# One expert's four result blocks share the tile that held its transposed rows, in place of two rotating buffers

## The chip, the cores and the metric

The kernel runs on one core of a Trainium2 chip. The metric is the time of one execution in microseconds (us), the median of repeated runs. A core has a matrix engine (PE, with its weight loads shown apart as PEld), a vector engine (DVE), an activation engine (ACT), GpSimd (POOL) and a queue engine (SP). Each runs its own list of instructions in order, and an instruction that must wait holds up all that stand behind it on its engine. DMA transfers are issued by SP and POOL and land later.

## The reference

Three stages follow one another: chunked attention, a mixture of experts that sends each of 4608 rows to one of eight experts, and a feed-forward stage with a rational activation.

```python
attn = softmax(scale * q_c @ k_c.T)            # chunks of 64
x    = (attn @ v_c) as rows                     # (4608, 512)
e    = argmax(x @ w_gate, axis=1)
for e in range(8):
    h = maximum(x[mask_e] @ w1[e], 0.0)         # 512 -> 1024
    out[mask_e] = gate_w * (h @ w2[e])          # 1024 -> 512
h = out @ w_in                                   # 512 -> 2048
g = (a0 + a1 h + a2 h^2 + a3 h^3) / (1 + |b0||h| + |b1| h^2 + 1e-6)
y = g @ w_out
```

## The kernel before

Rows are handled in tiles of 128. Each expert e takes the first 512 of its rows, in four tiles j = 0 to 3; what an expert has beyond 512 is worked through by `Extra` objects of 128 rows, one of them woven into each expert (`ex`, called `late` once the next expert has begun). Every matrix product is made of three passes over a value split into a high and a low part (`mm3`), so a group of four 128-deep steps is 12 matmuls.

The rows of an expert are gathered by POOL (`g`), transposed on PE, and written by ACT (high part) and DVE (low part) into `xT`, a tile of 16 KB per partition (`prep_x`, called as `p(j)`). There are two places for it, the pools `xt_p[0]` and `xt_p[1]`, and expert e uses `xt_p[e % 2]`; so `xT` of expert e+1, written in the middle of expert e, takes the place that expert e-1 used. `first(c)` makes 128 of the 1024 hidden values for all 512 rows, `relu(c)` moves them out on ACT and DVE as `hT`, and `second(c)` adds their part to four accumulators in PSUM, `yp[0..3]`. `xT` is read for the last time in `first(7)`.

`out(j)` copies `yp[j]` out of PSUM, on DVE for j = 0 and 2 and on ACT for j = 1 and 3, and POOL then scatters the 128 rows to `ys` in DRAM by an indirect DMA. The copy goes to a buffer of the pool `o_p`, which has two buffers that are used in turn; the results of the `Extra` objects (`yos`) and a small work tile for their indices (`extra_idx`) take theirs from the same two. `out(0)` and `out(1)` stand at the end of expert e, `out(2)` behind `first(0)` and `out(3)` behind `first(1)` of expert e+1. The last expert calls all four at its end, and the third and fourth then take buffers of `xg_p`, a pool of three that the gathered rows and the hidden values of the `Extra` (`hrs`) share:

```python
    for j in range(4):
        cur.second(6, (j,))
        cur.second(7, (j,))
        weight(V)
        cur.out(j, j > 1)
```

The order of the instructions on PE, DVE and ACT in this part is that of the program text (a manual schedule). POOL and SP are ordered by the framework's planner, which also puts in the waits. `weight()` splits a block of weights that SP has loaded into its parts (ACT, then DVE); `convert(1)` does half of a conversion of the last stage's weights on DVE. After the experts, `load_rows(0)` reads the first 512 rows of `ys` back into `xt_p[1]`, and the feed-forward stage begins.

Of the kernel before, what the change touches and what calls it, by code (L numbers as in the profile page):

```python
# [9 lines left out]
F32 = mybir.dt.float32  # L10
# [32 lines left out]
def kernel(  # L43
# [31 lines left out]
    xt_p = [ctx.enter_context(tc.tile_pool(name="xt_a", bufs=1))]  # L75
# [155 lines left out]
    def weight(eng=None):  # L231
        raw, tag, ws, c, nm, deint = raws.pop(0)
        ws[c] = split_w(raw, tag, nm, deint,
                        eng or alternate(c if type(c) is int else c[1]))
        ahead()
# [9 lines left out]
    def scatter(idx, o, alone=False):  # L245
        d = nc.gpsimd.indirect_dma_start(
            out=ys, out_offset=bass.IndirectOffsetOnAxis(ap=idx, axis=0), in_=o, in_offset=None)
        if not alone:
            tc.declare_no_dep(d.ins, group="ys", reason="each place has a row of its own")
            tc.add_to_no_dep_group("ys", d.ins)  # L250
# [14 lines left out]
    def new_x(e):  # L265
        return xt_p[e % 2].tile([128, 2, 4, 512], F32R, tag="xt", name=f"xT{e}")
# [34 lines left out]
    def new_out(nm, spare):  # L301
        if spare:
            return xg_p.tile([128, 512], F32, tag="xg", name=nm)
        return o_p.tile([128, 512], F32, tag="o", name=nm)
# [4 lines left out]
    class Extra:  # L309


        def __init__(self, idx, weights, nm, xt=None):
            self.idx, self.nm, self.xt = idx, nm, xt
            self.own = xt is None
            self.w1s, self.w2s = weights
            self.hts, self.hrs = [], []
# [40 lines left out]
        def out(self):  # L357
            o = new_out(f"yo{self.nm}", False)
            nc.scalar.activation(o, self.yp, AF.Copy)
            scatter(self.idx[:, 0:1], o, self.nm == "d")  # L360

    class Expert:


        def __init__(self, e, xt, weights, n):
            self.e, self.xt, self.n = e, xt, n
            self.w1s, self.w2s = weights
            self.yp, self.hts, self.hps = None, {}, {}

        def first(self, c):  # L370
            w = 128 * self.n
# [21 lines left out]
                mm3(self.yp[j], lambda x: ht[:, x, 128 * j:128 * j + 128],  # L393
                    lambda y: w[:, y, i0:i0 + 512], c == 0, c == 7)

        def out(self, j, spare=False):
            o = new_out(f"yo{self.e}_{j}", spare)
            if j % 2:
                nc.scalar.activation(o, self.yp[j], AF.Copy)
            else:  # L400
                V.tensor_copy(o, self.yp[j])
            scatter(sidx[:, self.e, j:j + 1], o)
# [83 lines left out]
    with man:  # L486
# [303 lines left out]
        cur = None  # L790
# [24 lines left out]
        for i in range(NTILE + 1):  # L815
# [64 lines left out]
            if i == X0:  # L880
                cur = Expert(0, new_x(0), (weights0[0:4], weights0[4:8]), EARLY // 128)
# [208 lines left out]
        xt = new_x(1)  # L1090
# [25 lines left out]
        old, cur = cur, Expert(1, xt, (w1s[1], w2s[1]), 4)  # L1116
# [38 lines left out]
        for e in range(1, NE):  # L1155
            nxt = e + 1 < NE
            if e > 1:
                old, cur = cur, Expert(e, xt, (w1s[e], w2s[e]), 4)
# [32 lines left out]
            if nxt:  # L1191
                xt = new_x(e + 1)
# [64 lines left out]
        for j in range(4):  # L1257
            cur.second(6, (j,))
            cur.second(7, (j,))
            weight(V)  # L1260
            cur.out(j, j > 1)


        rows0 = list(load_rows(0))
# [95 lines left out]
```

## Time and profile before

| | |
|---|---|
| median of 3 runs | 1517.3 us (1515.2 to 1517.8) |
| the profiled execution, its own time | 1519.63 us |
| its span, from the first to the last instruction | 1517.2 us |
| mean granted PE clock over the span | 0.989 |
| PE busy | 1463.4 us (96%) |
| DVE busy | 1270.8 us (84%) |
| ACT busy | 926.3 us (61%) |
| POOL busy | 447.9 us (30%) |

The profiled execution took 2.43 us more than its span, and 2.3 us more than the median. Attention fills the first 200 us, the experts the time to about 690 us, the feed-forward stage the rest. Busy shares are averages over these stages; PE's share counts matmuls from start to modelled end, which overlap.

### The profile page before, as it was taken

To read this page: it belongs to the slowest core of one execution; us is meant where nothing else is said; L and a number is where in the kernel's file an instruction comes from. 1 tells how busy PE (TensorE), PEld (TensorE's weight loads), DVE (VectorE), ACT (ScalarE), POOL (GpSimd) and SP (SyncE) were. 2 spreads that over 40 slices of the span, in tenths; PEclk is the share of its full clock that TensorE was granted. 3 is DMA by queue.
4 is the path that set the end of the run, shared out by engine and by line. 5 is a ranking of instruction groups with operands and counts; after the bars stand their busy time and mean duration, and the time that the engine had idled before them with its cause. 6 is when DMAs were issued, how large, how long until landed. Compare 5 with 4: busy or idle time off the path is not lost. (4 is left out here: it accounts for less than half of the span.)

```text
span 1517.2 us, 22399 instructions
## 1 busy us (share of the span) xinstructions
PE 1463.4 (96%) x7812; PEld 1198.8 (79%) x7812; DVE 1270.8 (84%) x2271; ACT 926.3 (61%) x1480; POOL 447.9 (30%) x415
## 2 busy tenths in 40 slices
PE   7999899999999999997899999999999999999998
PEld 5787788877778777876678888888888888888886
DVE  4888776988989889975989888888888888888886
ACT  5888544543444434544667667676776766667675
POOL 5565532121121211112642323222222222222232
PEclk9999999999999999999999999999999999999999
DMA  8999636776767878762301000010100001000000
GB/s 215 250 261 282 175 113 211 249 248 232 256 221 240 252 224 263 226 210 80 97 17 54 1 29 21 0 53 4 42 14 29 29 1 49 8 35 1 28 1 28
DMA packets 122897, 180.07 MB, mean 119 GB/s; under 512 B 51872, under 2 KB 78496, under 8 KB 122784
## 3 DMA queue, kind: packets, MB, share of 16 engines
q1 hardware_dynamic: 112352, 148.20, 32.6%
q0 software_dynamic: 10432, 30.44, 5.6%
q8 instruction: 62, 1.02, 0.3%
q14 instruction: 51, 0.42, 0.1%
HBM read 140.68 MB, written 37.91 MB: 118 GB/s over the span
## 5 line engine op out<-in xcount | busy, mean ns | idle before, releaser
L262 PE MATMUL f<-yT,wf 128*128 128x512 f32 x1728 | 412.8, 390 | 5.7 <-DVE t L449 2.2
L262 PE MATMUL z<-wf,g 128*128 128x512 f32 x1680 | 405.8, 392 | 9.5 <-POOL g L462 4.7
L262 PEld LDWEIGHTS f<-yT,wf 128*128 128x128 f32 x1728 | 323.2, 188 | 74.2 <-DVE t L449 2.7
L262 PEld LDWEIGHTS z<-wf,g 128*128 128x128 f32 x1680 | 314.6, 189 | 77.6 <-POOL g L462 6.4
L462 POOL TENSOR_TENSOR g<-t,g 128x512 fp32r<-128x512 f32 x140 | 209.6, 1498 | 521.3 <-ACT g L461 504.6
L262 PE MATMUL h<-xT,w 128*128 128x512 f32 (+1 forms) x768 | 187.6, 394 | 12.2 <-DVE hT L382 12.2
L262 PE MATMUL y<-w,hT 128*128 128x512 f32 x744 | 183.8, 395 | 0.0
L262 PEld LDWEIGHTS h<-xT,w 128*128 128x128 f32 x768 | 145.7, 193 | 41.9 <-DVE hT L382 14.5
L446 DVE TENSOR_TENSOR t<-t,f 128x512 f32<-128x512 f32 x144 | 98.5, 684 | 90.5 <-ACT u L445 90.0
L448 ACT ACTIVATE u<-t,cq 128x512 f32<-128x512 f32 x144 | 104.6, 726 | 92.0 <-DVE t L447 91.6
L447 DVE SCALAR_TENSOR_TENSOR t<-t,co,u 128x512 f32<-128x512 f32 x144 | 158.9, 1104 | 0.0
L262 PEld LDWEIGHTS y<-w,hT 128*128 128x128 f32 x744 | 136.9, 188 | 27.8 <-issue 0.4
L461 ACT ACTIVATE g<-t 128x512 fp32r<-128x512 f32 x140 | 89.0, 636 | 102.9 <-DVE t L453 102.8
L443 ACT ACTIVATE t<-f,co 128x512 f32<-128x512 f32 x144 | 112.0, 778 | 34.4 <-PE f L262 17.7
L381 ACT ACTIVATE hT<-h 128x512 fp32r<-128x512 f32 (+1 forms) x64 | 37.4, 584 | 148.7 <-PE h L262 106.9
L453 DVE SCALAR_TENSOR_TENSOR t<-t,co 128x512 f32<-128x512 f32 x144 | 125.3, 870 | 2.0
L451 DVE SCALAR_TENSOR_TENSOR t<-t,u 128x512 f32<-128x512 f32 x144 | 102.2, 710 | 15.4 <-ACT u L450 15.4
L452 DVE SCALAR_TENSOR_TENSOR t<-t,u 128x512 f32<-128x512 f32 x144 | 109.1, 758 | 0.5
L445 ACT ACTIVATE u<-f,co 128x512 f32<-128x512 f32 x144 | 98.4, 683 | 14.0 <-DVE t L452 9.8
L449 DVE SCALAR_TENSOR_TENSOR t<-t,co,f 128x512 f32<-128x512 f32 x144 | 106.3, 739 | 0.0
L450 ACT ACTIVATE u<-u 128x512 f32<-128x512 f32 x144 | 90.5, 629 | 2.2
L444 ACT ACTIVATE t<-f 128x512 f32<-128x512 f32 x144 | 85.1, 591 | 0.0
(203 smaller groups left out, 1981.1 us busy)
## 6 DMA issues: line engine op xcount, KB each, us to landing
raw_w<-in_moe_w_dram SPq DMA_DIRECT2D x64, 512.0 KB
raw_s<-in_moe_w_dram SPq DMA_DIRECT2D x64, 512.0 KB
v<-in_v_dram SPq DMA_DIRECT2D x144, 64.0 KB
xs<-x POOLq DMA_DIRECT2D x36, 256.0 KB
out_dram<-o SPq DMA_DIRECT2D x36, 256.0 KB
raw<-in_moe_w_in_dram SPq DMA_DIRECT2D x32, 256.0 KB
raw<-in_moe_w_out_dram SPq DMA_DIRECT2D x32, 256.0 KB
yg<-ys SPq DMA_DIRECT2D x32, 256.0 KB
```

Source lines behind the costliest of these rows:

```text
L262: nc.tensor.matmul(o, lhsT=lhs(x), rhs=rhs(y), start=(first and n == 0), stop=(last and n == 2))
L443: nc.scalar.activation(p, hp, AF.Identity, scale=a3, bias=a2)
L445: nc.scalar.activation(vv, hp, AF.Abs, scale=b0)
L446: V.tensor_tensor(out=p, in0=p, in1=hp, op=ALU.mult)
L447: V.scalar_tensor_tensor(qq, qq, b1, vv, op0=ALU.mult, op1=ALU.add)
L448: nc.scalar.activation(r, qq, AF.Abs_reciprocal_sqrt, bias=cq)
L449: V.scalar_tensor_tensor(p, p, a1, hp, op0=ALU.add, op1=ALU.mult)
L450: last_act = nc.scalar.activation(r, r, AF.Square).ins
L451: V.scalar_tensor_tensor(qq, qq, CQ, r, op0=ALU.add, op1=ALU.mult)
L452: V.scalar_tensor_tensor(qq, qq, -2.0, r, op0=ALU.add, op1=ALU.mult)
L453: V.scalar_tensor_tensor(p, p, a0, qq, op0=ALU.add, op1=ALU.mult)
L462: nc.gpsimd.tensor_tensor(out=gt[:, 1], in0=p, in1=gt[:, 0].bitcast(F32), op=ALU.subtract)
```

## The change

`out(j)` no longer takes a buffer of `o_p` or `xg_p`. The first `out` of an expert asks the pool `xt_p[e % 2]` for a tile of [128, 4, 512] under the same tag as `xT`, that is, for the place of the expert's own `xT`, and each of the four copies writes its quarter of it.

```diff
-            self.yp, self.hts, self.hps = None, {}, {}
+            self.yp, self.ot, self.hts, self.hps = None, None, {}, {}
...
-        def out(self, j, spare=False):
-            o = new_out(f"yo{self.e}_{j}", spare)
+        def out(self, j):
+
+            if self.ot is None:
+                self.ot = xt_p[self.e % 2].tile([128, 4, 512], F32, tag="xt", name=f"yo{self.e}")
+            o = self.ot[:, j]
             if j % 2:
                 nc.scalar.activation(o, self.yp[j], AF.Copy)
...
-            cur.out(j, j > 1)
+            cur.out(j)
```

PE, DVE, ACT and SP keep the order of their instructions; what differs on them is the waits. On DVE, at the end of expert 1 and the start of expert 2, the rows were these (a `waits` note names the semaphores: DMASW are those of POOL's DMAs, DMAHW those of SP's):

```order
L401 COPY yo_0_4453<-y_0_3897 128x512 [waits DMASW4_49,DMASW2_49]
L177 TENSOR_SCALAR cv_4459<-raw_55_4381 128x256 [waits DMAHW6_49,DMAHW5_49]
L178 TENSOR_SCALAR cv_4459<-cv_4459 128x256 [waits DVE_49]
L179 TENSOR_SCALAR cv_4459<-cv_4459 128x256 [waits DVE_49]
L180 SCALAR_TENSOR_TENSOR cv_4459<-raw_55_4381,cv_4459 128x256 [waits DVE_49]
L401 COPY yo_2_4479<-y_2_3899 128x512 [waits DMASW5_49,Activation_49]
L140 TENSOR_TENSOR s_2_0_4482<-raw_s_2_0_4336,s_2_0_4482 128x1024 [waits DMAHW3_49,PE_49,Activation_49]
```

In the change the same place on DVE reads:

```order
L404 COPY yo_4451<-y_0_3895 128x512
L177 TENSOR_SCALAR cv_4456<-raw_55_4379 128x256 [waits DMAHW6_49,DMAHW5_49]
L178 TENSOR_SCALAR cv_4456<-cv_4456 128x256 [waits DVE_49]
L179 TENSOR_SCALAR cv_4456<-cv_4456 128x256 [waits DVE_49]
L180 SCALAR_TENSOR_TENSOR cv_4456<-raw_55_4379,cv_4456 128x256 [waits DVE_49]
L404 COPY yo_4451<-y_2_3897 128x512
L140 TENSOR_TENSOR s_2_0_4478<-raw_s_2_0_4334,s_2_0_4478 128x1024 [waits DMAHW3_49,PE_49,Activation_49]
```

The two copies stand where they stood, without a wait. The waits for scatters are found at a later place instead: where ACT and DVE write the first tile of the `xT` that takes the place next.

POOL is the one engine whose order differs. From the last gather of expert 1's middle (`xgs`) to that of expert 2's, it was:

```order
L240 DMA xgs_4207<-xs,ixs_3985 128x512
L240 DMA xg_0_4689<-xs,gidx 128x512
L240 DMA xg_1_4691<-xs,gidx 128x512
L246 DMA ys<-yo_1_4456,sidx 45568x512
L246 DMA ys<-yo_0_4453,sidx 45568x512
L240 DMA xg_2_4693<-xs,gidx 128x512
L246 DMA ys<-yo_2_4479,sidx 45568x512
L246 DMA ys<-yo_3_4518,sidx 45568x512
L246 DMA ys<-yos_4609,ixs_3985 45568x512
```

and is now:

```order
L240 DMA xgs_4205<-xs,ixs_3983 128x512
L246 DMA ys<-yo_4451,sidx 45568x512
L240 DMA xg_0_4684<-xs,gidx 128x512
L240 DMA xg_1_4686<-xs,gidx 128x512
L246 DMA ys<-yo_4451,sidx 45568x512
L240 DMA xg_2_4688<-xs,gidx 128x512
L246 DMA ys<-yo_4451,sidx 45568x512 x2
L246 DMA ys<-yos_4604,ixs_3983 45568x512
```

The scatter of the block that ACT copies (j = 1) has moved ahead of two gathers for expert 3, and the scatters of j = 2 and 3 have changed places.

At the end of the last expert, ACT's rows for the `Extra`'s hidden values are another place where waits differ. Before:

```order
L399 ACTIVATE yo_3_7759<-y_3_7475 128x512 [waits PE_49]
L340 ACTIVATE hrs_0_7778<-hs_0_7765 128x512 [waits DMASW5_49,DMASW4_49,PE_49]
L138 ACTIVATE wf_6_7793<-raw_wf_6_7719 128x1024 [waits DMAHW6_49]
L340 ACTIVATE hrs_1_7796<-hs_1_7780 128x512 [waits DMASW5_49,PE_49,Activation_49]
L257 ACTIVATE hTs_0_7798<-htps_0_7799 128x512 [waits DVE_49,PE_49]
```

and in the change:

```order
L402 ACTIVATE yo_7701<-y_3_7455 128x512 [waits PE_49]
L340 ACTIVATE hrs_0_7755<-hs_0_7742 128x512 [waits PE_49]
L138 ACTIVATE wf_6_7770<-raw_wf_6_7699 128x1024 [waits DMAHW6_49]
L340 ACTIVATE hrs_1_7773<-hs_1_7757 128x512 [waits PE_49]
L257 ACTIVATE hTs_0_7775<-htps_0_7776 128x512 [waits DVE_49,PE_49]
```

Here nothing has moved; the two `hrs` wait for PE alone, since no result block stands in their pool.

## Rows read from the trace of the kernel before

**Rows 1.** The page's first part: busy us, share of the span, instructions.

```profile
PE 1463.4 (96%) x7812; PEld 1198.8 (79%) x7812; DVE 1270.8 (84%) x2271; ACT 926.3 (61%) x1480; POOL 447.9 (30%) x415
```

**Rows 2.** Who waited for whom, PE, 192 to 760 us: total us, times, longest.

```profile
PE h L262 <- DVE hT L382: 12.2, 5, 3.3
...
PE xtp L256 <- DVE xT L258: 1.7, 3, 1.3
PE htps L256 <- ACT hrs L340: 1.5, 1, 1.5
```

**Rows 3.** The same list for DVE, 200 to 700 us, its two longest.

```profile
DVE yo L401 <- DMA ys<-yo,sidx: 24.3, 6, 5.3
DVE s L140 <- ACT s L138: 5.2, 4, 3.1
```

**Rows 4.** Timeline, expert 1 to 2: start us, us, engine, line; in brackets idle before.

```profile
312.46 0.98 POOL L246 DMA_INDIRECT ys<-yo,sidx  x1 [0.62 <-DVE cv L177]
...
317.90 0.69 DVE L401 COPY yo<-y 128x512 f32<-128x512 f32 x1 [4.32 <-DMA ys<-yo,sidx]
...
320.88 1.15 POOL L246 DMA_INDIRECT ys<-yo,sidx  x1 [0.30 <-ACT hT L381]
321.10 0.68 DVE L382 SCALAR_TENSOR_TENSOR hT<-h,hT 128x512 fp32r<-128x512 f32 x1
...
321.84 3.01 PE L262 MATMUL h<-xT,w 128*128 128x512 f32 x12 [2.31 <-DVE hT L382]
...
327.41 2.88 PE L262 MATMUL y<-w,hT 128*128 128x512 f32 x12
...
338.99 0.59 ACT L257 ACTIVATE xT<-xtp 128x512 fp32r<-128x512 f32 x1
```

**Rows 5.** Timeline, DVE and PE, expert 2 to 3 and 3 to 4.

```profile
380.25 0.69 DVE L401 COPY yo<-y 128x512 f32<-128x512 f32 x1 [4.29 <-DMA ys<-yo,sidx]
...
384.19 4.46 PE L262 MATMUL h<-xT,w 128*128 128x512 f32 x12 [2.25 <-DVE hT L382]
...
391.40 2.88 PE L262 MATMUL y<-w,hT 128*128 128x512 f32 x12
...
441.99 0.69 DVE L401 COPY yo<-y 128x512 f32<-128x512 f32 x1 [3.84 <-DMA ys<-yo,sidx]
...
445.93 4.62 PE L262 MATMUL h<-xT,w 128*128 128x512 f32 x12 [1.76 <-DVE hT L382]
```

**Rows 6.** Stretches, first and last of four: us, busy by engine, PEclk, DMA, GB/s.

```profile
382.00:392.00 10.00, 7.81 (x27) 6.28 (x28) 9.73 (x21) 3.25 (x5) 2.07 (x2) 0.83 0.79 251
...
569.00:580.00 11.00, 8.05 (x28) 6.50 (x29) 10.69 (x22) 4.29 (x7) 2.84 (x2) 0.84 0.78 237
```

**Rows 7.** Timeline, DVE, expert 6 to 7.

```profile
627.74 0.69 DVE L401 COPY yo<-y 128x512 f32<-128x512 f32 x1 [1.84 <-DMA ys<-yo,sidx]
```

**Rows 8.** Timeline, end of the experts, before the feed-forward stage.

```profile
679.99 0.88 SPq L708 DMA_DIRECT2D yg<-ys  x2
680.04 0.60 ACT L340 ACTIVATE hrs<-hs 128x512 f32<-128x512 f32 x1 [2.47 <-DMA ys<-yo,sidx]
...
681.18 7.62 PE L262 MATMUL ys<-s,hTs 128*128 128x512 f32 x24
...
684.11 1.67 DVE L714 TENSOR_SCALAR yg<-yg,gate 128x512 f32<-128x512 f32 x4
...
688.64 1.91 PE L256 MATMUL ytp<-ident,yg 128*128 128x128 f32 x16
```

**Rows 9.** Timeline, end of expert 0.

```profile
236.51 3.02 PE L262 MATMUL hr<-w,xT 128*128 128x512 f32 x12
...
238.09 0.68 DVE L401 COPY yo<-y 128x512 f32<-128x512 f32 x1
...
240.68 1.29 DVE L258 TENSOR_TENSOR xT<-xtp,xT 128x512 fp32r<-128x512 f32 x2 [1.91 <-ACT xT L257]
```

## Prediction, before the run

> **What bounds the kernel now.** I began with the page's busy times. PE is at 96% [rows 1], so only what makes PE idle or slow can be won, and the stage decides which wait that is. The list of PE's waits between 192 and 760 us, the expert stage with its two edges, comes next: the longest entry is `h` waiting for DVE's `hT`, 12.2 us in five pieces [rows 2]. DVE's own list for that stage shows why DVE was late: its largest entry by far is the copy `yo` waiting for the scatter of an earlier `yo`, 24.3 us at six places [rows 3]. The timeline puts the two together. At the change from expert 1 to 2, POOL starts a scatter at 312.46 and DVE's copy of block 2, which needs the buffer that this scatter reads, starts only at 317.90, after 4.32 us of idling; behind it in DVE's list stand a weight split, a half conversion and then `hT` of chunk 0, at 321.10; and PE, whose third `first` needs the PSUM buffer that this `hT` frees, idles 2.31 us and goes on at 321.84 [rows 4]. So the reader is to see one chain, scatter, copy, `hT`, `h`, at each expert boundary.
>
> Two more things are seen after the wait. At the next boundary the 24 matmuls that follow it run from 384.19 to 391.40, 7.21 us [rows 5], while the same 24 at the first boundary ran from 321.84 to 327.41, 5.57 us [rows 4]: 1.64 us more. The granted clock explains it: over such a stretch it averages 0.83 or 0.84, where the stage otherwise has the full 2.4 GHz [rows 6]; the first and the last of four such boundaries stand there. PE fell to its lower level of 1.2 GHz after idling. The third thing is the end of the stage, where ACT waits 2.47 us for a scatter before it can write `hrs` [rows 8], because blocks 2 and 3 of the last expert sat in `xg_p`; PE waits 1.5 us for that [rows 2].
>
> DVE is nearly as full as PE here. From the copy at 380.25 to that at 441.99 it needs 61.74 us, of which 3.84 are the wait: 57.9 us of work per expert. PE from 384.19 to 445.93 also takes 61.74 us; without the 1.76 us wait and 1.64 us of slow clock it is 58.3 us [rows 5]. Both must be kept in view: a gain on PE beyond what DVE can follow would not come.
>
> **The change, part by part.** Durations come from the profiled execution: span 1517.2 us, own time 1519.63 us, 2.3 us above the median of 1517.3 us; I carry the difference over to the median.
>
> *The waits of the copies go.* The order shows the DVE and ACT copies without any wait in the change. Without 4.32 us of idling `hT` would have been ready about 4.3 us sooner, well before PE needed it 2.31 us sooner. The last boundary says the same: there the stall is 1.84 us [rows 7], and none of PE's five waits belongs to it, so about 2 us of lateness cost nothing. I take all five waits as gone: 12.2 us [rows 2].
>
> *The slow clock after four of them.* 1.64 us at the one worked out, four times 6.6 us; the stretches give 10.00 x 0.17 = 1.7 and 11.00 x 0.16 = 1.8 each, 7.0 in all [rows 6]. I take 6.6 us; the lower bound is nothing, if the clock falls elsewhere. On this the Trainium skill's page "TensorE: Matmul & The Clock Gate" (Part 1) speaks against counting on it: it says that the monitor's time base runs freely and that one kernel shows a different number of slow matmuls from run to run. By that rule the 6.6 us may stay, and the sum would be smaller by them. The trace agrees in part: the first boundary's 2.31 us wait, longer than the 1.76 us one, brought no fall.
>
> *The transposes that waited for DVE.* Three waits of `xtp` for `xT`, 1.7 us [rows 2], come where DVE is behind in the middle of an expert. DVE gains 4.3 us per boundary and PE about 2.3 + 1.6 = 3.9 us, so DVE is a little less behind than before. Bounds 0 and 1.7 us; I take 1.5 us, nearest to their removal.
>
> *The end of the stage.* `hrs` no longer shares a pool with result blocks: the 1.5 us wait goes. The 24 matmuls behind it took from 681.18 to 688.64, 7.46 us [rows 8], 1.9 us above the 5.57 us: slow clock again. Together 3.4 us, bounds 1.5 and 3.4. What PE does next needs the rows `yg`, scaled by DVE from 684.11 for 1.67 us; PE would come to them at 685.2 with the first of the four ready, so it is just covered; if the cover fails, up to 0.6 us return. The load of `yg` now waits for all of the last expert's scatters; it started at 679.99 and ACT was released by one of the last of them at 680.04, so the load is late by little, and SP has nothing urgent behind it.
>
> *Waits that are added.* First, the tile of expert e-1's results must be scattered before `xT` of expert e+1 may overwrite it. The last scatter of a boundary starts at 320.88; the one at 312.46 had released its reader after 5.44 us; so the place is free at about 326.3 and the first write to it is ACT's at 338.99 [rows 4], 12.7 us later. Cost nothing. Second, the copies may not start before `xT` is last read. From expert 1 on that was `first(7)`, several groups back. In expert 0 the rest block reads it in the 12 matmuls from 236.51, until about 239.5, and DVE's copy stood at 238.09: it is 1.4 us later, and DVE idled 1.91 us behind it anyway, waiting for ACT [rows 9]. Nothing. Third, POOL's first two gathers for the next expert but one now stand behind one scatter more, but still ahead of the one that started at 312.46; their rows are transposed shortly before the `xT` write at 338.99 [rows 4], so some 25 us cover them. The copies themselves have the same size and engine.
>
> *Friction.* With both engines at about 58 us per expert, PE may meet DVE at new places. Above: a wait as long as the longest `xtp`, 1.3 us, at six experts, 7.8 us; below: none, as at the last boundary. I take 1.2 us, near the lower.
>
> Sum: 12.2 + 6.6 + 1.5 + 3.4 - 1.2 = 22.5 us. DVE's limit, 24.3 us in the stage and 3.4 us at its end, lies above that. The span would be 1494.7, its own time 1497.1, the median 1517.3 - 22.5 = 1494.8 us.
>
> **The rivals.** *The clock keeps falling elsewhere.* The stage has little slack, so small waits remain and falls come with them: 6.6 and 1.9 us stay, the gain is 14.0 us, 1503.3 us. For it: a 1.5 us wait was enough at the stage's end. Against it: the long stretches between boundaries, with their short `xtp` waits, show none.
>
> *DVE becomes the bound in many small pieces.* Friction at its upper end instead of 1.2 us: gain 15.9 us, 1501.4 us; for it speak 57.9 against 58.3 us.
>
> *Another wait takes the place of the copies'.* Behind the copy stands a weight split, which needs ACT's part and a load. If the loads were late, DVE would stop there for the same 4 us and the time would stay within 0.2% of 1517.3 us, the least that a measurement of this kernel can tell from no change. Against it: DVE waited for ACT's split only 5.2 us at four places in 500 us [rows 3], and DMA is busy 79% even behind a stall [rows 6].
>
> *Slower.* The first write of the next `xT`, on ACT and then DVE, now waits for scatters. It decides from the point where a scatter takes 5.4 + 12.7 = 18.1 us to land; each us beyond costs six experts one each, so 22.5 / 6 = 3.8 us more, 21.9 us, makes the change slower; at 24 us it would be 1494.8 + 6 x 5.9 = 1530 us. Against it: the six stalls, which end with a landing each, are 5.3 us at most [rows 3].
>
> *More than forecast.* DVE's limit reached in full, 27.7 us: 1489.6 us.
>
> **How the numbers follow.** Forecast (1490 to 1499) 0.58; clock falls elsewhere 0.17; DVE in small pieces 0.12; another wait instead 0.04; slower 0.04; more than forecast 0.05. The predicted time is 1495 us. The range 1489 to 1506 takes in the forecast, both middle rivals and DVE's limit, 0.9 of the chance; I keep it that wide because the two unknown sizes, clock and friction, can add. Faster by over 0.2%: 0.92; same 0.04; slower 0.04.
>
> **What would show it.** Right: no DVE or ACT `yo` waiting for a scatter; the entry of `h` for `hT` gone or under 2 us; the expert period near 58 us; full clock over each boundary; `hrs` released by PE. Wrong: slow clock at new places (first rival), many waits of `h` or `xtp` for DVE (second), `s` splits waiting for a load (third), ACT's or DVE's first `xT` waiting for `ys<-yo` (slower).

## The result, and the profile after

The changed kernel takes **1495.55 us** (median of 4 runs, 1494.40 to 1496.19) against 1516.28 us for the kernel before, timed beside it (4 runs, 1515.20 to 1517.80): a ratio of 0.9873, 95% interval 0.986 to 0.9886. It is 20.7 us faster; the forecast was 1495 us. The profiled execution of the changed kernel took 1494.4 us with a span of 1492.4.

First the page's busy times, which answer to [rows 1]:

```profile
PE 1455.7 (98%) x7812; PEld 1193.5 (80%) x7812; DVE 1268.9 (85%) x2271; ACT 924.4 (62%) x1480; POOL 446.4 (30%) x415
```

The instructions are as many as before, on every engine. PE is busy 7.7 us less with the same 7812 matmuls: its mean granted clock is 0.995 where it was 0.989. The rest of the gain is idle time that is gone.

The list of PE's waits between 192 and 760 us answers to [rows 2] (total us, times, longest):

```profile
PE xtp L256 <- DVE xT L258: 0.9, 5, 0.2
PE htps L256 <- ACT hrs L340: 0.2, 1, 0.2
```

The entry of `h` for `hT`, 12.2 us before, isn't there any more; `xtp` went from 1.7 to 0.9 us, `htps` from 1.5 to 0.2. One entry grew: `hr` waits 1.3 us for ACT's `xT` at 230 us, where it waited 0.5 for DVE. That is ahead of the first copy of a result, and the second profiles of the two kernels have 0.7 us before and 0.4 after, so the change is not its cause. DVE's list from 200 to 700 us answers to [rows 3]:

```profile
DVE yg L717 <- DMA yg<-ys: 10.9, 2, 10.7
DVE hT L382 <- ACT hT L381: 6.7, 4, 4.6
DVE s L140 <- ACT s L138: 6.5, 9, 3.0
...
DVE yo L404 <- PE hr L262: 1.4, 1, 1.4
```

No copy waits for a scatter. The first line belongs to the feed-forward stage; its like before came at 703.6 us, outside this window. The last line is the new wait that the prediction priced at 1.4 us and at nothing in time: expert 0's copy waits until the rest block has read `xT`. The timeline of the boundary from expert 1 to 2 answers to [rows 4] (start us, us, engine, line; idle time before in brackets):

```profile
308.50 1.00 POOL L246 DMA_INDIRECT ys<-yo,sidx  x1 [24.07 <-ACT yo L402]
...
312.31 0.68 DVE L404 COPY yo<-y 128x512 f32<-128x512 f32 x1
312.41 0.99 POOL L246 DMA_INDIRECT ys<-yo,sidx  x1 [0.30 <-PE h L262]
...
315.51 0.68 DVE L382 SCALAR_TENSOR_TENSOR hT<-h,hT 128x512 fp32r<-128x512 f32 x1
...
316.76 2.01 POOL L246 DMA_INDIRECT ys<-yo,sidx  x1 [0.30 <-issue]
318.33 2.88 PE L262 MATMUL h<-xT,w 128*128 128x512 f32 x12
...
335.35 0.59 ACT L257 ACTIVATE xT<-xtp 128x512 fp32r<-128x512 f32 x1
```

Read it from the copy of block 2, at 312.31: nothing stands in brackets, and the scatter that it used to wait for starts only after it, at 312.41. `hT` starts at 315.51, 2.8 us before PE's third group `h`, which starts at 318.33 right behind the matmuls ahead of it. The added wait is the last line: ACT writes the next `xT` at 335.35 without idling, 18.6 us after the last scatter of a block started. The 24.07 us that POOL idles are harmless: it has nothing else to do.

At the end of the stage, which answers to [rows 8]:

```profile
656.74 0.60 ACT L340 ACTIVATE hrs<-hs 128x512 f32<-128x512 f32 x1 [1.18 <-PE hs L262]
...
657.88 5.99 PE L262 MATMUL ys<-s,hTs 128*128 128x512 f32 x24
...
658.58 0.89 SPq L711 DMA_DIRECT2D yg<-ys  x2
...
663.37 0.88 DVE L717 TENSOR_SCALAR yg<-yg,gate 128x512 f32<-128x512 f32 x2 [2.48 <-SPq L1291]
...
663.96 2.20 PE L256 MATMUL ytp<-ident,yg 128*128 128x128 f32 x16
...
675.33 10.09 PE L262 MATMUL f<-yT,wf 128*128 128x512 f32 x36 [1.99 <-issue]
```

`hrs` is released by PE, and the 24 matmuls of `ys` take 6.08 us to the start of `ytp` instead of 7.46. But the load of `yg` is issued 0.70 us after their start, where it was issued 1.19 us ahead of it, and DVE gets the rows late. How late is told by the second profile of the kernel before, where the rows were there in time and the same matmuls ran at full rate: 5.85 us from the start of `ys` to that of `ytp`, 0.2 less than in the change.

```profile
679.04 6.01 PE L262 MATMUL ys<-s,hTs 128*128 128x512 f32 x24
...
684.89 1.91 PE L256 MATMUL ytp<-ident,yg 128*128 128x128 f32 x16
```

The slow group is now the 36 matmuls of `f`: 10.09 us, and 8.47 in the trace of before.

**Where the time came from.** One cut through both traces separates the parts. Stretch S1 goes from the second-half `ys` of the Extra in expert 1 (272.25 us before, 271.22 after) to that in expert 7, and so over the six boundaries that had a stall (that from expert 0 to 1 lies ahead of it); S2 from there to `ytp`. For the kernel before, by stretches (us, busy time by engine, PEclk, DMA share, GB/s):

```profile
core 0: us, PE busy (x) PEld busy (x) DVE busy (x) ACT busy (x) POOL busy (x), PEclk, DMA share, GB/s
272.25:634.54 362.29, 348.40 (x1574) 283.18 (x1572) 327.06 (x688) 161.81 (x214) 68.50 (x58) 0.98 0.75 241
634.54:688.64 54.10, 52.56 (x230) 42.77 (x229) 40.78 (x70) 23.50 (x30) 6.00 (x5) 0.97 0.66 211
```

And for the change:

```profile
271.22:612.53 341.31, 340.44 (x1574) 279.01 (x1573) 328.64 (x690) 161.42 (x214) 68.09 (x58) 1.00 0.79 257
612.53:663.96 51.43, 51.09 (x229) 41.53 (x228) 38.26 (x66) 23.29 (x31) 6.58 (x5) 1.00 0.65 215
```

The spans differ by 24.8 us: 1.0 ahead of 272 us, 21.0 in S1, 2.7 in S2, 0.1 behind. The 1.0 us is no gain of the change: it is there at 230 us already, ahead of the first copy of a result, and the second pair of profiles, shown further down, has none of it. In S1 PE's waits fell from 13.9 to 0.9 us and its busy time by 8.0 us at a granted clock of 1.00 instead of 0.98. That looks like the prediction's sum, waits plus slow clock. The experiments show that it should be read in another way.

### The profile page after: what moved, and what is told of

Read it like the earlier page. It is cut to its first block, busy times and chain, and to the rows that moved or that the text cites. A ratio compares the mean times of both kernels' runs of the same rounds, so it can differ in the third digit from the quotient of the medians.

```text
span 1492.4 us, 22391 instructions
## 1 busy us (share of the span) xinstructions
PE 1455.7 (98%) x7812; PEld 1193.5 (80%) x7812; DVE 1268.9 (85%) x2271; ACT 924.4 (62%) x1480; POOL 446.4 (30%) x415
## 4 chain that ended last, share of the span: by engine, by line
PE 46%; DVE 3%; issue 2%; ACT 1%; POOL 1%; DMA 0%; SPq 0%; ACTq 0%; POOLq 0%
PE z L262 23%; PE f L262 23%; PE ytp L256 1%; DVE t L450 1%; DVE t L455 1%; DVE t L456 1%; DVE t L454 1%; POOL wf L140 1%; POOL g L465 1%; DMA yg<-ys 0%; DVE t L452 0%; ACT u L448 0%; ACT u L451 0%; ACT t L447 0%; DVE t L449 0%
## 5 line engine op out<-in xcount | busy, mean ns | idle before, releaser
L465 POOL TENSOR_TENSOR g<-t,g 128x512 fp32r<-128x512 f32 x140 | 209.2, 1495 | 521.6 <-ACT g L464 455.0
L262 PE MATMUL h<-xT,w 128*128 128x512 f32 (+1 forms) x768 | 180.9, 384 | 0.0
L262 PEld LDWEIGHTS h<-xT,w 128*128 128x128 f32 x768 | 142.4, 188 | 26.4
L448 ACT ACTIVATE u<-f,co 128x512 f32<-128x512 f32 x144 | 98.3, 683 | 14.8 <-DVE t L455 10.9
L246 POOL DMA_INDIRECT ys<-yo,sidx x31 | 39.6, 1277 | 193.2 <-ACT yo L402 155.0
```

Of the source, the lines that this page charges most:

```text
L262: nc.tensor.matmul(o, lhsT=lhs(x), rhs=rhs(y), start=(first and n == 0), stop=(last and n == 2))
L448: nc.scalar.activation(vv, hp, AF.Abs, scale=b0)
L465: nc.gpsimd.tensor_tensor(out=gt[:, 1], in0=p, in1=gt[:, 0].bitcast(F32), op=ALU.subtract)
```

## Experiments

The two theories at the outset: the copy's wait for a scatter costs all of it (the prediction), or it is the order on POOL and the place of the results. A third question came with e5 and e6: which engine sets the expert's period before, and which after.

**e1: blocks 2 and 3 alone in the place of `xT`.**

```diff
+            if j < 2 and self.e < NE - 1:
+                o = new_out(f"yo{self.e}_{j}", False)
...
+            if j > 1 or self.e == NE - 1:
+                o = self.ot[:, j]
```

> Only blocks 2 and 3 of experts 0 to 6 go to the place of xT; blocks 0 and 1 keep the two rotating buffers of the kernel before, so that no copy of a boundary has to wait for a scatter of the same boundary, while the gathers on POOL stand in the order of the kernel before. Theory (the gain comes from the copy's wait alone): the time of the change, 1495.6 us, within 1493 to 1499; DVE's copy of block 2 without a wait, PE's h without one. Rival (it is POOL's order of scatters and gathers that the change sets free): most of the gain is gone, 1510 us or more.

Measured: 1497.12 us (4 runs, 1494.42 to 1499.36), ratio 0.9889, interval 0.9872 to 0.9905; S1 is 341.47 us. The gain is whole, and POOL's gathers and scatters at the boundary stand as before, so their order is not what was set free. It is enough that two of the four blocks have places of their own.

**e2: only the last expert; e3: all but the last.** e2 takes the new place where `self.e == NE - 1` and `new_out(..., False)` elsewhere; e3 the reverse, with `new_out(..., j > 1)` for the last expert.

> Only the last expert's results go to the place of xT; experts 0 to 6 keep the two rotating buffers. This is the end of the stage by itself. Theory: 2.7 us (what the two traces show from the last expert's first group to ytp) to 3.4 us (the prediction's term) below the kernel before: 1513 to 1513.6 us against 1516.3. Rival (the slow clock after the 1.5 us wait only moves to a later place): 1.5 us or nothing, 1514.8 to 1516.3. The five waits of h for hT stay, about 12 us.

> Experts 0 to 6 put their results in the place of xT, the last one keeps the rotating buffers and the spare ones of the rows' pool. Theory: the 21.0 us that the two traces show over the boundaries are all won, less nothing: 1516.3 - 21.0 = 1495.3, to 1498.5 us with the end of the stage as in the kernel before (its hrs wait of 1.5 us back on PE). Rival (the parts are not additive, because what PE wins at the boundaries is waited for at the end): 1500 us or more.

Measured: e2 1515.82 us (10 runs, 1511.73 to 1519.15), ratio 1.0012, interval 0.9999 to 1.0025: nothing won. e3 1497.20 us (4 runs), ratio 0.9886, interval 0.987 to 0.9903: all but nothing lost, with the 1.2 us wait of `htps` for `hrs` back on PE. So the six boundaries are the gain, and the end of the stage, 3.4 us in the prediction, isn't to be told from nothing. e3's S2 is 52.18 us with the old end of the stage: PE waited there, but the clock did not fall after it, and the 24 matmuls took 6.02 us.

**e4: the new place, but two blocks rotating in it.**

```diff
-                self.ot = xt_p[self.e % 2].tile([128, 4, 512], F32, tag="xt", name=f"yo{self.e}")
-            o = self.ot[:, j]
+                self.ot = xt_p[self.e % 2].tile([128, 2, 512], F32, tag="xt", name=f"yo{self.e}")
+            o = self.ot[:, j % 2]
```

> The change, but the tile in the place of xT holds two blocks instead of four, so that blocks 2 and 3 overwrite blocks 0 and 1 and their copies wait again for the scatters of these; POOL's order is that of the change. Theory (the number of places for results decides): the stall of DVE's copy is back, 4 to 5 us at each boundary, with waits of h for hT on PE and falls of the granted clock behind them: about 1513 us, within 1508 to 1520. Rival (where the results lie and the order on POOL decide): 1496 us.

Measured: 1525.63 us (4 runs, 1524.39 to 1529.37), ratio 1.0085, interval 1.0068 to 1.0102: slower than the kernel before. DVE's list of waits in e4:

```profile
DVE yo L404 <- DMA ys<-yo,sidx: 30.2, 6, 6.0
```

The stall is back, and with it all of the gain is lost: the number of places decides, not where they lie. Its size was missed: 30.2 us at six boundaries where the kernel before has 24.3 [rows 3]. Half of the difference lies at the last boundary, where the copy waits 4.80 us against 1.84 [rows 7]. Why a scatter keeps the next copy waiting longer here is not shown; S1 is longer by about that much (368.83 against 362.29, 6.5 us).

**e5: all four copies on ACT.**

```diff
-            if j % 2:
-                nc.scalar.activation(o, self.yp[j], AF.Copy)
-            else:
-                V.tensor_copy(o, self.yp[j])
+            nc.scalar.activation(o, self.yp[j], AF.Copy)
```

> The change, with all four copies of a boundary on ACT; DVE has two copies of 0.69 us less per expert, ACT two more. Theory (PE is the bound of the expert stage after the change: 58.3 us per expert, 299.1 us busy of 300): the time of the change, 1495.6 within 2 us. Rival (DVE is the bound, 288.7 of 300 us busy, and PE only follows it): 1.4 us per expert less, about 1487 us.

Measured: 1495.96 us (4 runs, 1493.04 to 1497.87), ratio 0.9856, interval 0.9833 to 0.9879, the same as the change. By stretches, S1 of e5:

```profile
274.60:615.87 341.27, 340.39 (x1574) 279.00 (x1572) 323.69 (x678) 167.40 (x226) 71.69 (x58) 1.00 0.80 258
```

DVE has 5 us less to do than in the change, and S1 is as long to 0.04 us: after the change PE sets the time.

**e6: the copy of block 2 made 3 times, and 8 times, on DVE in experts 1 to 6.**

```diff
-                V.tensor_copy(o, self.yp[j])
+                for _ in range(8 if j == 2 and 0 < self.e < NE - 1 else 1):
+                    V.tensor_copy(o, self.yp[j])
```

> The change, with the copy of block 2 on DVE made three times instead of once in experts 1 to 6: 2 x 0.69 = 1.4 us more DVE work at each of six boundaries, with no wait added. Theory (a lateness of DVE of up to about 2 us there costs PE nothing at the boundary, as at the last boundary of the kernel before; but DVE has only some 0.4 us per expert to spare, 57.9 against 58.3): about 1 us per expert, 1500 us, within 1496 to 1503. Rival (DVE has slack enough): 1495.6 us within 1 us.

> The change, with the copy of block 2 on DVE made eight times instead of once in experts 1 to 6: 7 x 0.69 = 4.8 us more DVE work at each of six boundaries, in the place of the 4.3 us wait of the kernel before and without any scatter to wait for. Theory (DVE's lateness at that place is the cause, whatever makes it late): the kernel before again or somewhat more, 1516 to 1521 us, with waits of h for hT of about 2 us on PE and clock falls behind them. Rival (lateness of DVE isn't what PE lost): 1496 us.

Measured: 1501.87 us (4 runs, 1498.53 to 1502.93; ratio 0.9894, interval 0.9871 to 0.9917) with 2 copies more, 1524.04 us (6 runs, 1521.88 to 1525.14; ratio 1.0044, interval 1.0029 to 1.0058) with 7. The second, on the timeline of DVE:

```profile
313.67 5.76 DVE L405 COPY yo<-y 128x512 f32<-128x512 f32 x8
```

And its S1 by stretches:

```profile
272.57:641.51 368.94, 348.75 (x1574) 283.04 (x1573) 356.55 (x732) 162.21 (x214) 63.73 (x58) 0.98 0.75 238
```

Eight copies take 5.76 us, one 0.68: 5.1 us more per boundary, in the place where the kernel before stalls 4.1. No scatter is waited for, yet PE waits for `hT` again (17.0 us at six places) and its clock is down to 0.98 again. So DVE's lateness alone makes both. The expectation was too low because it took PE's losses over from before; DVE's surplus gives it: six times 5.1 is 30.5 us, less some 3 us that DVE has to spare, 27.5 on top of 1495.55 is 1523. The run with two more says how much is to spare: 6 x 1.46 = 8.8 us added, S1 longer by 5.5 (346.82 against 341.31), 3.3 us hidden, 0.55 per expert.

**e7: the last expert's results in the other place.** The tile comes from `xt_p[(self.e + (self.e == NE - 1)) % 2]`, which no later load shares.

> The change, but the last expert's results go to the other of the two places of xT, which no later load shares with them, so that the load of the rows yg need not wait for that expert's scatters. Theory (the load is 0.6 us late in the change and PE stands 0.5 us within the 24 matmuls of ys and behind them): the load starts about 0.6 us sooner, the 24 matmuls and the wait behind them together take 0.5 us less, time 1495.1 us. Rival (the load is not what ends PE's wait, or the time is lost again behind it): 1495.6 us, no change.

Measured: 1496.82 us (5 runs, 1493.20 to 1497.88), ratio 0.986, interval 0.9839 to 0.9882: no difference from the change that these runs can tell. End of the stage in e7's timeline:

```profile
660.36 6.00 PE L262 MATMUL ys<-s,hTs 128*128 128x512 f32 x24
660.37 0.88 SPq L711 DMA_DIRECT2D yg<-ys  x2
...
666.20 1.97 PE L256 MATMUL ytp<-ident,yg 128*128 128x128 f32 x16
```

The load is issued with the first matmul of `ys`, 0.7 us sooner than in the change's first profile and 0.2 sooner than in its second. `ytp` starts 5.84 us after `ys`, which these had at 6.08 and 5.85; the 23 matmuls of `f` behind `ytp` start 9.69 us after `ys` instead of 9.95 and 9.96. So some 0.3 us of the expected 0.5 are seen, in one profile, too little for the times to show.

**e8 and e9: seven matmuls more in PE's wait, before and after the change.** By now all traces of S1 pointed to one rule: before, S1 is about 338 us plus DVE's stalls, whatever PE does. e8 tests it against the prediction's account by filling PE's idle time, to see whether its clock then stays up and what that is worth. The added result is overwritten.

```diff
                 late.y(0)
                 weight()
                 convert(1)
+                if nxt:
+                    cur.yp = new_acc(f"y{e}", 4)
+                    for _ in range(7):
+                        nc.tensor.matmul(cur.yp[0], lhsT=cur.w1s[0][:, 0, 0:128],
+                                         rhs=cur.xt[:, 0, 0, :], start=True, stop=True)
                 cur.first(2)
```

> The kernel before, with seven matmuls more at each of the five boundaries 1 to 2 up to 5 to 6, between ys of the first half and the group h that waits for hT: 7 x 0.227 = 1.6 us of work whose result is overwritten, put where PE idles 1.76 to 3.3 us. Theory A (the prediction's account: PE's waits and the slow clock behind them are both costs, added up): PE idles so little there that its clock stays up, and the 6.6 to 8 us of slow clock are won: 1508 to 1510 us. Theory B (formed after the runs so far: DVE sets the expert's period, 338 us of its own from the first boundary to the last plus its waits for scatters; PE's waits and its slow clock only fill the rest): no change, 1516 us within 2; where the clock stays up PE waits longer instead.

> The change, with the same seven matmuls more at the same five boundaries, whose result is overwritten. Theory (PE is the bound there now): 5 x 1.6 = 7.9 us more, 1503.5 us, within 1502 to 1505. Rival (DVE is still the bound and PE has room): 1496 us.

Measured: e8 1515.62 us (10 runs, 1511.45 to 1517.69) against 1515.01 for the kernel before beside it, ratio 0.9997, interval 0.9985 to 1.001: no change. In PE's timeline:

```profile
319.59 1.75 PE L1176 MATMUL y<-xT,w 128*128 128x512 f32 x7
322.21 3.06 PE L262 MATMUL h<-xT,w 128*128 128x512 f32 x12 [0.87 <-DVE hT L382]
```

PE's other wait in S1 of e8:

```profile
PE xtp L256 <- DVE xT L258: 7.1, 10, 1.2
```

And S1 of e8 by stretches:

```profile
272.42:633.49 361.07, 350.57 (x1609) 285.04 (x1607) 327.66 (x689) 164.14 (x214) 66.95 (x58) 1.00 0.76 242
```

The reader is to see four things. The wait of `h` is down to 0.87 us, the clock is 1.00 over the whole of S1, 35 matmuls more are done, and S1 is still 361 us. The time that they and the faster clock took out of one wait came back in another: `xtp` waits 7.1 us for DVE's `xT`, where it waited 1.7. The slow clock was taken away and nothing was won. This settles it against the prediction's account: in the kernel before the slow clock cost no time of its own.

e9: 1501.70 us (4 runs, 1500.31 to 1503.38), ratio 0.9913, interval 0.9894 to 0.9931; S1 347.51 us, 6.2 longer than in the change, PE busy through all of it. What cost nothing before costs 6.2 us now, since PE is the bound. It is less than 7.9 us: the 0.9 us of `xtp` waits went, and 0.8 us stay open.

**Both kernels once more, with a profile each.**

> The kernel before once more, for a second profile. Theory B: the stretch from the first boundary to the last is 338 us plus DVE's waits for scatters, whatever PE's waits and clock do in it; theory A: it follows PE's waits plus its slow time. The part after the experts: either the 24 matmuls of ys run slow again (7.6 us, S2 54.1) or they don't (6.0 us, about 52.2).

> The change once more, for a second profile: 341.3 us from the first boundary to the last, full clock there, and 51.2 to 51.5 us from there to ytp.

Measured: 1515.86 and 1495.95 us, one run each. By stretches, the kernel before a second time:

```profile
272.24:632.80 360.56, 345.58 (x1574) 280.85 (x1572) 327.67 (x689) 163.36 (x214) 66.99 (x58) 0.99 0.76 242
632.80:684.89 52.09, 50.95 (x229) 41.64 (x228) 40.21 (x69) 23.68 (x30) 6.00 (x5) 1.00 0.67 216
```

And the change a second time:

```profile
272.24:613.50 341.26, 340.41 (x1573) 279.02 (x1572) 328.66 (x690) 161.73 (x214) 67.84 (x58) 1.00 0.80 257
613.50:664.71 51.21, 50.96 (x229) 41.64 (x228) 38.57 (x66) 23.30 (x30) 6.58 (x5) 1.00 0.66 213
```

The spans of this pair differ by 19.6 us: 19.3 in S1, 0.9 in S2, and 0.6 given back behind. The S1 of before moved by 1.7 us between its two profiles, and so did its stalls (24.3 and 21.9 us, 2.4 less); that of the change stayed within 0.05.

All kernels in one table, in us. DVE's stall is its wait for scatters from the list of waits (for e8 with 1.4 us of the same copies put down to ACT), for e6 the copies added.

| kernel | S1 | PE waits | PE busy | PEclk | DVE stall or added work | S1 less that | S2 |
|---|---|---|---|---|---|---|---|
| before | 362.29 | 13.9 | 348.40 | 0.98 | 24.3 | 338.0 | 54.10 |
| before, again | 360.56 | 14.9 | 345.58 | 0.99 | 21.9 | 338.7 | 52.09 |
| e2 | 360.49 | 14.8 | 345.66 | 0.99 | 22.6 | 337.9 | 51.62 |
| e8 | 361.07 | 10.5 | 350.57 | 1.00 | 22.5 | 338.6 | 52.52 |
| e4 | 368.83 | 17.5 | 351.31 | 0.97 | 30.2 | 338.6 | 53.41 |
| e6, 7 more | 368.94 | 20.2 | 348.75 | 0.98 | 30.5 | 338.4 | 51.25 |
| e6, 2 more | 346.82 | 5.4 | 341.44 | 1.00 | 8.8 | 338.0 | 51.72 |
| after | 341.31 | 0.9 | 340.44 | 1.00 | 0 | 341.3 | 51.43 |
| after, again | 341.26 | 0.8 | 340.41 | 1.00 | 0 | 341.3 | 51.21 |
| e1 | 341.47 | 0.9 | 340.53 | 1.00 | 0 | 341.5 | 51.19 |
| e3 | 341.66 | 1.1 | 340.58 | 1.00 | 0 | 341.7 | 52.18 |
| e5 | 341.27 | 0.9 | 340.39 | 1.00 | 0 | 341.3 | 51.21 |
| e7 | 341.30 | 0.9 | 340.42 | 1.00 | 0 | 341.3 | 51.19 |
| e9 | 347.51 | 0.0 | 347.51 | 1.00 | 0 | 347.5 | 51.21 |

The seventh column is the finding. In the first seven rows, with seven different sums of PE's waits and clock, S1 is 338.3 us within 0.4 plus what DVE lost: DVE's list is the bound there. DVE's waits within S1 say the same: before, the six for scatters are the only entry, so nothing that PE does holds DVE up, and what is left, 362.29 - 327.06 - 24.3 = 10.9 us, is some 16 ns between each two of its 688 instructions; e8 leaves 10.9 us too. In the last seven rows S1 is PE's busy time within 1.1. The kernel is the longer of the two, and the change let DVE's list sink below PE's.

## Why the prediction was right, and where its account was not

The time, the place and the first cause were right: the copies waited for scatters, two more places for results took that wait away (e1, e4), and nothing took its place. The sum was 22.5 us and the medians gave 20.7. That the time came out within 0.8 us of 1494.8 all the same is in part luck: the kernel before ran 1.0 us faster beside the change than the 1517.3 that the sum was taken from. By its steps:

- *The waits of the copies, 12.2 us.* All five waits of `h` went, as forecast.
- *The slow clock after four of them, 6.6 us.* This is the step that failed as an account. PE's busy time in S1 did fall by 8.0 us in the first pair of profiles and by 5.2 in the second, but e8 shows that a full clock alone wins nothing before the change: S1 was DVE's list, and a slow PE only waited less. Waits and slow clock came out near the gain because together they are what DVE's stalls left over PE's own time: 13.0 + 8.0 = 21.0, and likewise 24.3 of stalls less the 3.3 us by which PE's 341.3 stands above DVE's 338.0. The second way needs no assumption on the clock. The prediction had its numbers, 57.9 against 58.3 us per expert, but used them as a limit only; its 24.3 us less six times 0.4 would have given 21.9 us for the boundaries.
- *The doubt about the clock.* The prediction weighed the Trainium skill's "TensorE: Matmul & The Clock Gate" (Part 1), by which one kernel shows another number of slow matmuls from run to run; the page says it of the start of a kernel. The runs show the like in the middle of one: the kernel before had four slow groups behind its boundary waits in one profile, two in the other. The time did not hang on it.
- *The transposes, 1.5 us, and friction, -1.2.* Together 0.3 forecast; `xtp` gave 0.8 us and no new wait came at the boundaries. The period is 58.27 us from one expert to the next, as two rows of `xtp` in the change show, where "near 58" stood:

```profile
463.42 0.66 PE L256 MATMUL xtp<-ident,xg 128*128 128x128 f32 x4 [0.18 <-DVE xT L258]
...
521.69 0.66 PE L256 MATMUL xtp<-ident,xg 128*128 128x128 f32 x4 [0.17 <-DVE xT L258]
```

- *The end of the stage, 3.4 us.* Too large. Some 2 us of it only this one execution had: S2 is 54.10 us in it, and 52.09 and 52.18 in the second profile of before and in e3, against 51.2 to 51.4 with the change. Of these 2 us 1.6 are the fall of the clock (7.46 us from `ys` to `ytp` instead of 5.85) and 0.4 a longer wait of `htps`. The prediction's 1.9 us for the clock measured these 24 matmuls by the 5.57 us of a boundary, which is not their full rate here. That leaves about 0.9 us, of which e2's time shows nothing. The cover for the load of `yg` failed by 0.2 us at `ytp`, where the prediction allowed up to 0.6.
- *The waits that are added.* None cost anything that the traces show. No scatter stands in ACT's waits from 270 to 640 us, nor in DVE's within S1, so no write of the next `xT` waited for the place.
- *From the profile to the median.* The 22.5 us were worked out on an execution of 1519.63 us and carried over whole to the median of 1517.3. Part of what made that execution long was part of the sum: its stalls were 2.4 us above those of the second profile and its S2 2.0 us. The second pair of profiles differs by 19.9 us in its own times.

The rivals: the clock did not fall elsewhere in the stage (1.00 in S1, both times), DVE did not become the bound in small pieces (e5), though only 0.55 us per expert keeps it from that (e6), and no load and no scatter took the copy's place.

## What to carry to other kernels

Where two engines are both nearly full, work out for each its own time over the same stretch, busy time, the short gaps between its instructions, and the waits that the other engine does not cause, and take the longer one; the gain from removing a stall on the first is that stall less the distance to the second. The follower's waits and its slow clock are no second cost to be added: lengthen or fill the follower's idle time, and if the total stays, it was not the bound. A buffer whose reader is a scatter came free here 5.2 to 6.7 us after the copy that filled it at five boundaries (312.18 to 317.90 us at the first) and 3.2 us after it at the last, so as many places as there are results in a burst are worth more than two in rotation, and a tile that is dead at that moment gives them for nothing.

## What had not been expected of the hardware

The length of a wait does not tell whether the clock falls behind it. In the kernel before, the same group `h` ran slow after waits of 1.76, 2.25, 2.61 and 3.30 us and at full rate after 2.31; in its second profile slow after 1.94 and 2.97, at full rate after 2.67. Two rows of that second profile, PE alone:

```profile
383.65 3.01 PE L262 MATMUL h<-xT,w 128*128 128x512 f32 x12 [2.67 <-DVE hT L382]
...
507.16 4.33 PE L262 MATMUL h<-xT,w 128*128 128x512 f32 x12 [1.94 <-DVE hT L382]
```

One run has six waits of nearly one length, e6 with 7 copies more: `h` idles 2.79 to 2.91 us before its groups, four of which ran slow (4.43 to 4.62 us) and two at full rate (3.02 us both, after 2.83 and 2.81).

Around the end of the stage the falls change place as well. The 24 matmuls of `ys` took 7.46 us to `ytp` in the first profile of before and 5.85 in its second. The 36 of `f` took 10.09 and 10.08 us in the first profile of the change and the second of before, and 8.47 in the other two. The 20 of `z` behind them, after a wait for ACT, took 6.45 and 6.43 us before and 5.52 and 7.50 with the change, where the next 20 of `z` in the change's second profile took 4.83.
